# Output transposes by row halves inside the next pair's 64-row block, masked probabilities 64 bytes into their tile, new phases of batch 2

## The chip, the cores and the metric

One core of a Trainium2 chip runs the whole program. Its engines are TensorE (PE in the profile; PEld is its weight load), VectorE (DVE), ScalarE (ACT), GpSimd (POOL) and SyncE (SP, which here only starts transfers). TensorE multiplies a stationary operand (loaded as weights) with a moving one and writes to PSUM, eight banks of 2 KB per partition; DVE and ACT copy results from there to SBUF.

The metric is the device time of one execution in microseconds: the median of several runs, and beside it one profiled execution, from which all durations below come.

## The reference

Sparse attention, then a feed-forward network. There are 8 batches of 8 heads, 576 positions, 64 channels per head. Heads 0 to 3 are local: query i sees keys i-31 to i. Heads 4 to 7 are strided: query i sees keys j <= i with j = i modulo 32.

```python
scores = scale * np.matmul(q, k.transpose(0, 1, 3, 2))
mask_local = (rel >= 0) & (rel < stride)          # stride 32, rel = i - j
mask_strided = (rel >= 0) & (pos[None, :] % stride == pos[:, None] % stride)
attn = softmax(where(mask, scores, -1e9));  y = np.matmul(attn, v)
x = y.transpose(0, 2, 1, 3).reshape(B * S, H * D)  # 4608 x 512
a = x @ w1;  b = x @ w2                            # 4608 x 1024 each
out = ((a * b) @ w3) @ w_out                       # 4608 x 512
```

## The kernel before

**Network.** w3 and w_out are folded into one matrix `w34` once. The 4608 tokens go in 9 tiles of 512 (`tch`). Per tile, `ab_parts` makes for each of 8 column blocks (jc) the product aps (4 matmuls of 512 columns), which ACT copies to asb, and bps (4 more), which DVE multiplies with asb into abt (L600). `o_parts` then multiplies abt with `w34` and ACT copies the result (osb, L651) to be stored. A unit is two matmuls: 32 units of ab and 16 of o in a tile. Tile 1 has 448 new columns in its ab units, because the first 64 are done earlier.

**Attention.** Heads go in pairs (two heads fill 128 channels), four pairs to a batch: i = 0 and 1 local, 2 and 3 strided; pair p belongs to batch p // 4. For batches 2 to 7 each pair p runs these steps:

- The block (`ph_TS`, scores L334, transposes L291 and L299). All of its matmuls contract over 64 rows, alternating between the lower and the upper row half of the array. First the scores of pair p, from `qT` and `kT`; then the transposes of the next pair's q and k. In the block that precedes a batch's first pair (`rest` true) also the last 64 rows of that batch's q and k, for all heads. Scores go to the PSUM tile sps (two banks), the last chunk and the transposes to pt (two banks). A local pair has six chunks of keys with 128, 96, 96, 96, 96 and 64 queries; a strided pair has four groups of 126 and one of 72, with the positions reordered by their remainder.
- `ph_soft`: ACT takes the exp (L359) of sps, then of pt; DVE multiplies with the mask into ptm (L348), a tile that lives throughout. After it come the copies of the next pair's qT and kT.
- `ph_PV` (L368): ptm as weights against v, which has a column of ones, back into sps; `norm` on DVE divides by the sums (L525, L526) into xqs.
- `ph_T2` (L535): whole-row transposes of xqs, five or six, into psM, a pool of one bank; then copies to `xT`, the network's input. A local pair's copy is one on DVE (L540), a strided pair's one on ACT and one on DVE (L547, L548).

**Order.** TensorE's order is written out; the other engines' instructions are placed by a planner, mostly in the order of the text. A list `stream` holds the steps with gaps between them, and `host` puts one network unit of the tile into each gap (in batch 2, before its last 24 gaps, 16 units into 18). Tile `tch` hosts batch `tch + 1`. Each pair is block, 6 gaps, PV, 5 gaps, T2, 1 gap, and a batch ends with its fourth pair; the next tile's ab units start there. The first block of batch 2 and five units are placed by hand ahead of that, with seven stream entries skipped.

Batches 0 and 1 run earlier, through functions whose names begin with `ah_`, and use `ph_T2` as well. PSUM is full: psF has 3 banks for the network, psB two tiles of two banks (sps and pt), psM one bank.

Of the kernel before, what the change touches and what calls it, by code (L numbers as in the profile page):

```python
# [19 lines left out]
def kernel(  # L20
# [11 lines left out]
    nc = tc.nc  # L32
# [19 lines left out]
    NR = S - NM  # L52
    KW = 640
    NB = 512
    LC = 384
    QL = (0, 128, 224, 320, 416, 512, S)
    QX = (0, 126, 252, 378, 504, S)
    PTW = 1280
    NW, NC, NQ = 144, 4, 640
    QN = (0, 144, 288, 432, 576, NQ)  # L60

# [23 lines left out]
    def copy(eng, out, in_):  # L85
        if eng == "a":
            return nc.scalar.copy(out=out, in_=in_)  # L87
        elif eng == "v":
# [1 line left out]
        return nc.gpsimd.tensor_copy(out=out, in_=in_)  # L90


    id16 = consts.tile([P, P], FP16)
    make_identity(nc, id16)


    maskL = consts.tile([P, S], FP16)
    maskX = consts.tile([XW, S], FP16)
    biasN = consts.tile([P, NQ], FP16)
    emb = consts.tile([P, 2, 640], FP16)  # L100
# [3 lines left out]
    nc.gpsimd.memset(causal, 1.0)  # L104
    nc.gpsimd.affine_select(out=causal, in_=causal, compare_op=ALU.is_ge,
                            fill=0.0, base=0, pattern=[[1, NW]], channel_multiplier=-1)
    setup["p"] = nc.gpsimd.affine_select(out=maskL[:, 0:P], in_=causal[:, 0:P], compare_op=ALU.is_ge,
                                         fill=0.0, base=31, pattern=[[-1, P]], channel_multiplier=1)
    nptms = [ffn.tile([P, 2, 2048], FP16, tag="abt", bufs=4, name="nptm0")]
    nc.gpsimd.memset(emb, 0.0)  # L110
# [6 lines left out]
                              in_=_ap(id16, 0, [[id16.ap[0][0], m], [0, n], [1, m]]))  # L117
        pe(nc.tensor.matmul(mps[0:w, lo:lo + n * m], sel[:, 0:w], sel, start=True, stop=True))
    for i in range(1, LT):
        nc.vector.tensor_copy(out=maskL[:, QL[i]:QL[i + 1]], in_=maskL[:, 32:32 + QL[i + 1] - QL[i]])  # L120
    maskN = tmp2[:, 0:NQ]
    nc.vector.memset(maskN[:, NC * NW:NQ], 0.0)
    nc.vector.tensor_mul(maskN[:, 0:NW], mps[:, 208:208 + NW], causal)
    nc.vector.tensor_mul(maskN[0:64, NC * NW:NQ], mps[0:64, 352:416], causal[0:64, 0:64])
    nc.vector.tensor_copy(out=maskN[:, NW:NC * NW].rearrange("p (c x) -> p c x", x=NW),
                          in_=_ap(maskN, 0, [[maskN.ap[0][0], P], [0, NC - 1], [1, NW]]))
    biasL = tmp[:, S:2 * S]
    for bias, mask in ((biasL, maskL), (biasN, maskN)):
        nc.vector.tensor_scalar(out=bias, in0=mask, scalar1=1.0, scalar2=BIG, op0=ALU.subtract, op1=ALU.mult)
# [144 lines left out]
    def rest_X(eng, t, pr):  # L274
        for g in range(2):
# [3 lines left out]
        copy(eng, t[:, 2:4, XC + 64:S].rearrange("x g (s c) -> x g s c", c=4),  # L279
             pr.rearrange("x g (s a c) -> x g s a c", s=2, c=4)[:, :, :, 7])  # L280

    def ph_T(s, rest, pt):
        ps = pt.bitcast(FP16)
        h0 = 2 * (s.hp % 2)
        for i, nm in enumerate("qk"):
            src = x16[(s.b, nm, s.hp // 2)]
            for c in range(4):
                c0 = i * 256 + c * 64
                for u in range(2):
                    r = half_rows(u)  # L290
                    pe(nc.tensor.transpose(ps[:, u, c0:c0 + 64],  # L291
                                           src[r, c, h0:h0 + 2].rearrange("p h d -> p (h d)"), id16[r, r]))
        if rest:
            src = x16[(s.b, "r")]
            for g in range(4):
                c0 = 512 + g * 64
                for u in range(2):
                    r = half_rows(u)
                    pe(nc.tensor.transpose(ps[:, u, c0:c0 + 64],  # L299
                                           src[r, 2 * g:2 * g + 2].rearrange("p h d -> p (h d)"), id16[r, r]))  # L300
        engs = (("a", qT), ("v" if s.local else "a", kT))

        def out():
            for i, (eng, t) in enumerate(engs):
                pi = ps[:, :, i * 256:i * 256 + 256]
                if s.local:
                    copy(eng, t[:, s.hp, 0:NM].rearrange("x (u p c) -> x u p c", u=2, c=4),
                         pi.rearrange("x u (c p) -> x u p c", c=4))
                else:
                    to = t[:, s.hp, 0:XC].rearrange("x (c w) -> x c w", w=XW)  # L310
                    for u in range(2):
                        copy(eng, to[:, :, 56 * u:56 * u + 56].rearrange("x c (t a) -> x c t a", a=7),
                             pi[:, u].rearrange("x (c t a) -> x c t a", c=4, a=8)[:, :, :, 0:7])
                    copy("v", t[:, s.hp, XC:XC + 64].rearrange("x (u t c) -> x u t c", u=2, c=4),
                         pi.rearrange("x u (c t a) -> x u t c a", c=4, a=8)[:, :, :, :, 7])
            if rest:
                for i, (eng, t) in enumerate((("a", qT), ("v", kT))):
                    pr = ps[:, i, 512:768].rearrange("x (g r) -> x g r", g=4)
                    copy(eng, t[:, 0:2, NM:S], pr[:, 0:2])
                    rest_X(eng, t, pr[:, 2:4])  # L320

        return out

    def ph_S(s):
        w, n, q = s.w, s.n, s.q
        sps = psB.tile([P, 2, NB], FP32, tag="big", name="sps")
        pt = psB.tile([P, 2, NB], FP32, tag="big", name="pt")
        s.ps = sps

        def sc(h, c):  # L330
            r = half_rows(h)
            l = q[c + 1] - q[c]
            o = sps[:, h, q[c]:q[c + 1]] if c < n - 1 else pt[:, h, LC:LC + l]
            pe(nc.tensor.matmul(o, kT[r, s.hp, w * c:w * c + P], qT[r, s.hp, q[c]:q[c + 1]],  # L334
                                start=True, stop=True))

        for i in range(n):
            sc(0, (i - 1) % n)
            sc(1, i)

        def soft():
            ph_soft(s, pt)

        return pt, soft

    def mask_mul(s, o, i, lo, hi, m):
        x = hi - lo
# [3 lines left out]
    def ph_soft(s, pt):  # L351
        kr, q, n = s.kr, s.q, s.n
        sps = s.ps
        pte = att.tile([P, 2 * S], FP16, tag="pte", bufs=2)
        ptm = s.ptm = ptms[s.hp % 2]
        pv = pte.rearrange("p (h x) -> p h x", h=2)
        m = q[n - 1]
        for lo, hi, src in ((0, m, sps[0:kr, 0:2, 0:m]), (m, S, pt[0:kr, :, LC:LC + S - m])):
            nc.scalar.activation(out=pv[0:kr, :, lo:hi], in_=src, func=AF.Exp, bias=0.0, scale=scale)  # L359
        mask_mul(s, ptm[0:kr, 0:2 * S], pte[0:kr], 0, S, 2)  # L360

    def ph_PV(s):
        n = s.n
        s.xqs = att.tile([P, LT, 2, D], FP16, tag="xqs", bufs=2, name="xqs")
        for c in range(n):
            for h in range(2):
                c0 = h * S + s.q[c]
                pe(nc.tensor.matmul(s.ps[:, h, c * 65:c * 65 + 65], s.ptm[0:s.kr, c0:c0 + P],  # L368
                                    s.v[0:s.kr, 2 * (s.hp % 2) + h, c, :], start=True, stop=True))
        norm(s, s.ps[0:s.kr, :, 0:n * 65], 0, n)  # L370

    def ah_T1(s, i, dst=None):
        if dst is None:
# [72 lines left out]
    def ah_scores(s, g, outs, kn, first):  # L446
        w, q = s.w, s.q
        cs, lo, hi = ah_group(s, g)
        for c in cs:
            for h in range(2):  # L450
                r = half_rows(h)
                mv = qT[r, s.hp, q[c]:q[c + 1]] if q[c] < S else \
                    qT[r, s.hp].rearrange("x (c w) -> x w c", w=NW)[:, P:NW]
                pe(nc.tensor.matmul(outs[h][0:kn, q[c] - lo:q[c + 1] - lo], kT[r, s.hp, w * c:w * c + kn],  # L454
                                    mv, start=first, stop=first or c == cs[-1]))

    def ah_bias(s, g, wide=True):
        kr = s.kr
# [60 lines left out]
        norm(s, xps[0:s.kr, :, 0:len(cs) * 65], cs[0], len(cs))  # L519

    def norm(s, xv, c0, l):
        w = s.kr
        rcp = att.tile([P, 2, LT], FP32, tag="rcp")
        xv = xv.rearrange("p h (i e) -> p h i e", e=65)
        nc.vector.reciprocal(out=rcp[0:w, :, 0:l], in_=xv[:, :, :, D])  # L525
# [3 lines left out]
    def ph_T2(s):  # L529
        n = s.n  # L530
        ps = psM.tile([P, 1024], FP16, tag="m")
        for t in range(n):
            l = max(min(s.q[t + 1] - s.q[t], P), YW)
            o = t * P if s.nat else s.q[t]
            pe(nc.tensor.transpose(ps[:, o:o + l],  # L535
                                   s.xqs[0:l, t].rearrange("p h d -> p (h d)"),
                                   id16[0:l, 0:l]))
        o = xT[s.hp][:, S * s.b:S * s.b + S]
        if s.local:
            copy("a" if s.b < AHEAD else "v", o, ps[:, 0:S])  # L540
        elif s.nat:
            nc.scalar.copy(out=o[:, 0:NM].rearrange("x (p c) -> x p c", c=4),  # L542
                           in_=ps[:, 0:NM].rearrange("x (c p) -> x p c", c=4))
            nc.vector.tensor_copy(out=o[:, NM:S], in_=ps[:, NM:S])
        else:
            ov = o.rearrange("x (t a c) -> x t a c", a=8, c=4)
            nc.scalar.copy(out=ov[:, :, 0:7], in_=ps[:, 0:XC].rearrange("x (c t a) -> x t a c", c=4, a=7))  # L547
            nc.vector.tensor_copy(out=ov[:, :, 7], in_=ps[:, XC:S].rearrange("x (t c) -> x t c", c=4))  # L548


    abts = {}
    fine = []
# [154 lines left out]
    def gaps(n):  # L707
        stream.extend([GAP] * n)

    def ph_TS(s, t):  # L710
        if s is not None:
            pt, soft = ph_S(s)
            after = [soft]
        else:
            pt = psB.tile([P, 2, NB], FP32, tag="big", name="pt")
            after = []
        if t is not None:
            after.append(ph_T(t, t.hp == 0, pt))
        for f in after:
            f()  # L720

# [72 lines left out]
    add(b3, 0, 1, 2, 3)  # L794
    batch_end[0] = len(stream)

    for p, s in enumerate(pairs):
        b, i = divmod(p, 4)
        if b < AHEAD:
            continue  # L800
        t = pairs[p + 1] if p + 1 < len(pairs) else None
        add(ph_TS, s, t)
        gaps(6)
        add(ph_PV, s)
        gaps(5)
        add(ph_T2, s)
        gaps(1)
        if i == 3:
            batch_end[b] = len(stream)
    pos = [0]  # L810

    def host(units, upto):
# [146 lines left out]
```

## Time and profile before

| what | value |
|---|---|
| median of 3 runs (275.81, 274.43, 275.63) | 275.63 us |
| profiled execution, time | 273.37 us |
| profiled execution, first to last instruction | 271.5 us |
| busy: PE, DVE, ACT, POOL | 260.0, 146.7, 147.1, 99.5 us |
| mean granted TensorE clock | 0.999 |
| first block of batch 2 | at 71.54 us |
| last output transposes | at 225.9 us |

Times in the profile count from the first instruction. A busy PE is not PE at its peak, since records of successive matmuls overlap: what a step costs PE is read from the start of its first matmul to the start of the next step's. In the timeline a line is a run of like instructions: start, length, engine, line, operation, output and inputs, sizes, count, and in brackets the idle time ahead of it with what ended it.

### The profile page before, as it was taken

The numbers are of one execution on the slowest core, as the hardware profiler recorded it, in microseconds if no ns is written. First come the engines' busy times: TensorE is split into PE (matmuls) and PEld (weight loads), VectorE is DVE, ScalarE is ACT, GpSimd is POOL, SyncE is SP. The second block draws the span as 40 slices with busy tenths as digits, with TensorE's granted clock in tenths as the row PEclk, the third lists the DMA queues.
The fourth block names the chain that finished last, engine by engine and source line by source line (L and its number), as shares of the span: only waits on it lengthen the run. The fifth ranks groups of instructions, "written<-read, shape, count | busy, mean of one in ns | idle before, by whom it ended". The sixth has DMA issues, their size and how long they took to land.

```text
span 271.5 us, 6432 instructions
## 1 busy us (share of the span) xinstructions
PE 260.0 (96%) x2516; PEld 139.1 (51%) x2516; DVE 146.7 (54%) x327; ACT 147.1 (54%) x311; POOL 99.5 (37%) x119
## 2 busy tenths in 40 slices
PE   2999999999999999999999999999999999999994
PEld 1764465655645555555555555555555554444442
DVE  6472543275777557745764765477647743321320
ACT  2773334678546656566566566656675644333322
POOL 5477776678438105711750175037300000000000
PEclk9999999999999999999999999999999999999999
DMA  7999999998797249627933992399320012012003
GB/s 207 281 358 394 393 410 294 233 257 234 204 304 210 107 142 256 188 96 249 255 100 118 239 245 83 125 266 223 109 116 2 0 43 114 0 41 116 0 27 129
DMA packets 61098, 48.65 MB, mean 179 GB/s; under 512 B 31804, under 2 KB 52492, under 8 KB 61068
## 3 DMA queue, kind: packets, MB, share of 16 engines
q1 hardware_dynamic: 57036, 40.97, 54.6%
q10 hardware_dynamic: 4032, 7.28, 7.0%
q8 instruction: 19, 0.31, 0.5%
q14 instruction: 11, 0.09, 0.1%
HBM read 38.80 MB, written 9.44 MB: 178 GB/s over the span
## 4 chain that ended last, share of the span: by engine, by line
PE 90%; DVE 4%; ACT 3%; issue 1%; DVEq 0%
PE ops L640 27%; PE aps L588 22%; PE bps L597 21%; PE ps L535 3%; PE sps L368 3%; PE pt L291 2%; PE sps L334 2%; PE tps L378 2%; PE sps L466 1%; PE sps L454 1%; PE pt L334 1%; PE trp L685 1%; DVE xqs L526 1%; PE xpl L511 1%; ACT xT L542 1%
## 5 line engine op out<-in xcount | busy, mean ns | idle before, releaser
L597 PE MATMUL bps<-xT,w2h 128*128 128x512 f16 (+1 forms) x288 | 74.5, 376 | 0.0
L588 PE MATMUL aps<-xT,w1h 128*128 128x512 f16 (+1 forms) x288 | 73.9, 377 | 0.5 <-ACT xT L542 0.5
L90 POOL CAST t<-st 128x1024 f16<-128x1024 f32 (+1 forms) x46 | 46.9, 1023 | 69.6 <-DMA st<-in_q_dram 46.0
L640 PE MATMUL ops<-w,abt 128*128 128x512 f16 x280 | 67.0, 379 | 0.0
L600 DVE TENSOR_TENSOR abt<-bps,asb 128x512 f16<-128x512 f32 (+1 forms) x72 | 48.6, 678 | 32.1 <-PE bps L597 29.6
L87 ACT COPY asb<-aps 128x512 f32<-128x512 f32 (+1 forms) x71 | 42.0, 593 | 44.0 <-PE aps L588 41.1
L588 PEld LDWEIGHTS <-w1h 128*128 128x128 f16 x288 | 26.2, 98 | 29.0 <-issue 1.0
L597 PEld LDWEIGHTS <-w2h 128*128 128x128 f16 x288 | 26.3, 98 | 27.1 <-issue 0.5
L640 PEld LDWEIGHTS <-abt 128*128 128x128 f16 x280 | 25.2, 98 | 25.8
L651 ACT COPY osb<-ops 128x512 f32<-128x512 f32 x35 | 20.6, 588 | 18.5 <-PE ops L640 17.4
L359 ACT ACTIVATE pte<-sps 128x1024 f16<-128x1024 f32 (+1 forms) x24 | 24.6, 1027 | 10.6 <-PE sps L334 10.6
L526 DVE TENSOR_TENSOR xqs<-sps,rcp 128x768 f16<-128x768 f32 (+1 forms) x24 | 21.4, 890 | 0.8
L348 DVE TENSOR_TENSOR ptm<-pte,maskL 128x1152 f16<-128x1152 f16 (+2 forms) x16 | 13.0, 820 | 12.6 <-ACT pte L359 12.3
L87 ACT COPY qT<-pt 128x224 f16<-128x224 f16 (+4 forms) x60 | 18.0, 362 | 2.1 <-ACT osb L651 2.1
L348 DVE TENSOR_TENSOR ptm<-pte,maskX 126x1152 f16<-126x1152 f16 x12 | 11.7, 972 | 13.6 <-ACT pte L359 13.6
L547 ACT COPY xT<-ps 128x504 f16<-128x504 f16 x12 | 6.9, 578 | 16.5 <-PE ps L535 16.5
L89 DVE COPY kT<-pt 128x512 f16<-128x512 f16 (+4 forms) x48 | 14.1, 325 | 3.3 <-ACT kT L87 1.6
L227 POOL CAST v16L<-st 96x768 f16<-96x768 f32 x16 | 13.2, 824 | 7.0 <-DMA st<-in_v_dram 3.6
L535 PEld LDWEIGHTS <-xqs 96*128 96x128 f16 (+3 forms) x176 | 11.6, 97 | 8.2 <-DVE xqs L526 1.7
L640 PE MATMUL ops<-woh,w3T 128*128 128x512 f16 x64 | 15.6, 379 | 0.0
L535 PE MATMUL ps<-id,xqs 96*128 96x96 f16 (+3 forms) x176 | 13.6, 210 | 1.0 <-DVE xqs L526 0.9
L368 PEld LDWEIGHTS <-ptm 128*128 128x128 f16 (+1 forms) x264 | 11.0, 98 | 6.4 <-DVE ptm L348 1.9
(112 smaller groups left out, 259.0 us busy)
## 6 DMA issues: line engine op xcount, KB each, us to landing
st<-in_q_dram SPq DMA_DIRECT2D x16, 512.0 KB, 5.0
st<-in_k_dram SPq DMA_DIRECT2D x16, 512.0 KB, 6.0
st<-in_moe_w_dram SPq DMA_DIRECT2D x16, 512.0 KB, 10.4
out_dram<-osb ACTq DMA_DIRECT2D x27, 256.0 KB, 2.0
st<-in_v_dram SPq DMA_DIRECT2D x32, 144.0 KB
st<-in_v_dram SPq DMA_DIRECT2D x24, 112.0 KB, 2.4
st<-in_moe_w_out_dram SPq DMA_DIRECT2D x4, 512.0 KB, 11.8
out_dram<-osb SPq DMA_DIRECT2D x8, 256.0 KB, 4.3
```

Of the source, the lines that this page charges most:

```text
L87: return nc.scalar.copy(out=out, in_=in_)
L90: return nc.gpsimd.tensor_copy(out=out, in_=in_)
L348: nc.vector.tensor_mul(o.rearrange("p (a x) -> p a x", x=x), i.rearrange("p (a x) -> p a x", x=x), _ap(s.mask, lo, [[s.mask.ap[0][0], s.kr ...
L359: nc.scalar.activation(out=pv[0:kr, :, lo:hi], in_=src, func=AF.Exp, bias=0.0, scale=scale)
L368: pe(nc.tensor.matmul(s.ps[:, h, c * 65:c * 65 + 65], s.ptm[0:s.kr, c0:c0 + P], s.v[0:s.kr, 2 * (s.hp % 2) + h, c, :], start=True, stop=True))
L526: nc.vector.tensor_mul(s.xqs[0:w, c0:c0 + l].rearrange("p i h d -> p h i d"), xv[:, :, :, 0:D], _ap(rcp, 0, [[rcp.ap[0][0], w], [LT, 2], [ ...
L535: pe(nc.tensor.transpose(ps[:, o:o + l], s.xqs[0:l, t].rearrange("p h d -> p (h d)"), id16[0:l, 0:l]))
L588: pe(nc.tensor.matmul(st["a"][:, 0:nt], w1h[:, ci, bass.ds(jc * P, P)], xT[ci][:, tok], start=(ci == 0), stop=(ci == KM - 1)))
L597: pe(nc.tensor.matmul(st["b"][:, 0:nt], w2h[:, ci, bass.ds(jc * P, P)], xT[ci][:, tok], start=(ci == 0), stop=(ci == KM - 1)))
L600: nc.vector.tensor_mul(abts[tch][:, jc, skip:], st["b"][:, 0:nt], st["asb"][:, 0:nt])
L640: pe(nc.tensor.matmul(st["ps"], lhs(ci), rhs(ci), start=(ci == 0), stop=(ci == KF - 1)))
L651: nc.scalar.copy(out=osb, in_=ps)
```

## The change

- `ph_T2` as a step of its own goes for all pairs of batches 2 to 7 but the last. In its place `ph_T2u` transposes the 64-row halves of the previous pair's xqs at the head of the next block: the lower half into the psM bank, the upper half into a free part of pt's second bank. Twelve half transposes for a local pair, ten for a strided one. The lower half's copy to xT is issued at once, the upper half's after the block. Copies are on DVE (a strided pair has four), except for the local pairs of batch 2, on ACT.
- For 64-row halves to hold whole groups, the rows are shifted. A local pair's first chunk is rotated, queries 32 to 127 before 0 to 31, so its score matmul is split in two (`q_parts`). A strided pair's weights in PV are read from one element earlier (28 for its last group), so its rows stand at 1 to 126; `norm` then covers 128 partitions. The masked probabilities start 32 elements (64 bytes) into ptm. The mask tile and the identity are widened to give the rotated order.
- The last 64 rows of q and k of batches 3 to 7 leave the block. A new step `ph_R` does them with four whole transposes into psM, three gaps after the fourth pair's PV, with four copies on ACT and four on DVE.
- The gaps: block, 6, PV, 6 for each pair; in batch 2 (8, 7), (7, 6), (5, 4), (5, 4). In a batch's fourth pair three of the second number lie ahead of `ph_R`. A batch now ends two gaps after the next batch's first block.

```diff
-    LC = 384
+    LC = 416
+    PT0 = 32
-    PTW = 1280
+    PTW = 1248
-    id16 = consts.tile([P, P], FP16)
+    idw = consts.tile([P, 2 * P - 32], FP16)
+    id16 = idw[:, 0:P]
-    maskL = consts.tile([P, S], FP16)
+    maskE = consts.tile([P, S + 32], FP16)
+    maskL = maskE[:, 32:S + 32]
...
+        lo = 0 if i == 1 else 32
+        nc.vector.tensor_copy(out=maskE[:, QL[i] + lo:QL[i + 1] + 32], in_=maskE[:, lo:32 + QL[i + 1] - QL[i]])
...
+    nc.vector.tensor_copy(out=idw[:, P:2 * P - 32], in_=id16[:, 0:P - 32])
...
+    def q_parts(s, c):
+        if s.local and c == 0:
+            return (32, P, 0), (0, 32, P - 32)
+        return (0, s.q[c + 1] - s.q[c], 0),
+
-    def ph_S(s):
+    def ph_S(s, r):
...
+        after = [ph_T2u(r, pt)] if r is not None else []
...
-            pe(nc.tensor.matmul(o, kT[r, s.hp, w * c:w * c + P], qT[r, s.hp, q[c]:q[c + 1]],
-                                start=True, stop=True))
+            for lo, hi, at in q_parts(s, c):
+                pe(nc.tensor.matmul(o[:, at:at + hi - lo], kT[r, s.hp, w * c:w * c + P],
+                                    qT[r, s.hp, q[c] + lo:q[c] + hi], start=True, stop=True))
...
-        mask_mul(s, ptm[0:kr, 0:2 * S], pte[0:kr], 0, S, 2)
+        mask_mul(s, ptm[0:kr, PT0:PT0 + 2 * S], pte[0:kr], 0, S, 2)
+
+    def row0(s, c):
+        return 0 if s.local else 1 if c < XN else 28
...
-                c0 = h * S + s.q[c]
+                c0 = PT0 + h * S + s.q[c] - row0(s, c)
...
+    def ph_T2u(s, pt):
+        o = xT[s.hp][:, S * s.b:S * s.b + S]
+        dst = [psM.tile([P, 1024], FP16, tag="m", name="t2a"), pt.bitcast(FP16)[:, 1, 512:1024]]
+
+        def tr(u, c, o):
+            r = half_rows(u)
+            pe(nc.tensor.transpose(dst[u][:, o:o + 64], s.xqs[r, c].rearrange("p h d -> p (h d)"), id16[r, r]))
+
+        if s.local:
+            tr(0, 0, 0)
+            tr(1, 0, 0)
+            for c in range(LT):
+                if c:
+                    tr(0, c, 64 * c)
+                if c + 1 < LT:
+                    tr(1, c, 32 * c + 64)
...
+        else:
+            for c in range(XN + 1):
+                for u in range(2):
+                    tr(u, c, 64 * c)
...
+        def out(u):
+            copy("a" if s.b == AHEAD and s.local else "v", outs[u], ins[u])
+            if tails:
+                nc.vector.tensor_copy(out=tails[u][0], in_=tails[u][1])
+
+        out(0)
+        return lambda: out(1)
+
+    def ph_R(b):
+        ps = psM.tile([P, 1024], FP16, tag="m", name="rps")
+        src = x16[(b, "r")]
+        for g in range(4):
+            pe(nc.tensor.transpose(ps[:, g * P:g * P + P], src[:, 2 * g:2 * g + 2].rearrange("p h d -> p (h d)"), id16))
+        pv = ps[:, 0:NM].rearrange("x (g i r) -> x i g r", g=4, i=2)
+        rest_copies([pv[:, 0], pv[:, 1]])
...
-            after.append(ph_T(t, t.hp == 0, pt))
+            after.append(ph_T(t, t.hp == 0 and t.b == AHEAD, pt))
...
+    GAPS = ((8, 7), (7, 6), (5, 4), (5, 4))
...
-        add(ph_TS, s, t)
-        gaps(6)
+        more = p + 1 < len(pairs)
+        g = GAPS[i] if b == AHEAD else (6, 6)
+        add(ph_TS, s, pairs[p + 1] if more else None, pairs[p - 1] if p > 4 * AHEAD else None)
+        gaps(2)
+        if i == 0:
+            batch_end[b - 1] = len(stream)
+        gaps(g[0] - 2)
         add(ph_PV, s)
-        gaps(5)
-        add(ph_T2, s)
-        gaps(1)
-        if i == 3:
-            batch_end[b] = len(stream)
+        gaps(3)
+        if i == 3 and more:
+            add(ph_R, b + 1)
+        gaps(g[1] - 3 if more else 2)
+    add(ph_T2, pairs[-1])
+    gaps(1)
+    batch_end[B - 1] = len(stream)
```

## The prediction

> **What bounds the kernel now.** I read the page's busy shares first, then the chain that ended last, then TensorE's timeline over single pairs, then the waits and the DVE and ACT timelines around the steps that move.
>
> ```profile
> PE 260.0 (96%) x2516; PEld 139.1 (51%) x2516; DVE 146.7 (54%) x327; ACT 147.1 (54%) x311; POOL 99.5 (37%) x119
> ...
> PE 90%; DVE 4%; ACT 3%; issue 1%; DVEq 0%
> ```
>
> TensorE (PE) is the bound: 90% of the chain. A cut counts only where PE issues less or waits less. The timeline of one local and one strided pair of batch 5, start and length in us:
>
> ```profile
> 154.37 0.43 PE L535 MATMUL ps<-id,xqs 128*128 128x128 f16 x6
> 154.63 0.60 PE L597 MATMUL bps<-xT,w2h 128*128 128x512 f16 x2
> 155.16 0.20 PE L334 MATMUL pt<-qT,kT 64*128 64x64 f16 x1
> ...
> 155.43 0.40 PE L291 MATMUL pt<-id,t 64*128 64x64 f16 x16
> 155.75 1.04 PE L588 MATMUL aps<-xT,w1h 128*128 128x512 f16 x4
> ...
> 168.39 0.39 PE L291 MATMUL pt<-id,t 64*128 64x64 f16 x16
> 168.62 0.28 PE L299 MATMUL pt<-id,t 64*128 64x64 f16 x8
> 168.84 2.76 PE L640 MATMUL ops<-w,abt 128*128 128x512 f16 x12
> 171.44 0.47 PE L368 MATMUL sps<-v16X,ptm 126*128 126x65 f16 x10
> 171.74 2.32 PE L640 MATMUL ops<-w,abt 128*128 128x512 f16 x10
> 173.90 0.42 PE L535 MATMUL ps<-id,xqs 126*128 126x126 f16 x5
> 174.16 0.60 PE L640 MATMUL ops<-w,abt 128*128 128x512 f16 x2
> ```
>
> Starts are what to compare, since records overlap. The output transposes (L535) cost 154.63-154.37 = 0.26 us, a strided pair's five also 0.26. Sixteen half-row transposes cost 168.62-168.39 = 0.23, or 14.4 ns each, because the two row halves run side by side. A 512-column product takes (173.90-171.74)/10 = 0.216, so a unit of two takes 0.43. Two of them after 154.63 end at 155.06 and the block starts at 155.16: entering the 64-row block costs 0.10. After it, eight halves (0.115) and the exit fill 168.62 to 168.84: another 0.10. The change leaves the number of blocks at 24.
>
> From batch 3 on PE never loses 0.12 us between two starts. Batch 2 is where it does:
>
> ```profile
> 76.06 0.54 PE L588 MATMUL aps<-xT,w1h 128*128 128x448 f16 x2
> 76.97 0.44 PE L535 MATMUL ps<-id,xqs 128*128 128x128 f16 x6 [0.36 <-DVE xqs L526]
> ...
> 79.84 0.54 PE L597 MATMUL bps<-xT,w2h 128*128 128x448 f16 x2
> 80.64 0.54 PE L368 MATMUL sps<-v16L,ptm 128*128 128x65 f16 x12 [0.26 <-DVE ptm L348]
> ...
> 82.15 0.92 PE L597 MATMUL bps<-xT,w2h 128*128 128x448 f16 x4
> 83.58 0.43 PE L535 MATMUL ps<-id,xqs 128*128 128x128 f16 x6 [0.51 <-DVE xqs L526]
> ```
>
> Here a 448-column product takes 0.188. Start to start the three lose 0.53, 0.42 and 0.68: 1.63 us together.
>
> **The change, part by part.** All sums are against the profiled execution, 273.37 us (span 271.5); it lies 2.26 below the median of the three runs, 275.63, and I carry the difference over to that median. About 0.5% (1.4 us) is what a measurement of this kernel can tell from no change.
>
> Output transposes. Twenty-three pairs (8 to 30: 12 local, 11 strided) lose a step of 0.26 and gain halves in the next block: 12 for a local pair (0.173, and 0.015 because the order begins with one half twice), 10 for a strided one (0.144). That is 12 x 0.072 + 11 x 0.116 = 2.14 us less. The last pair keeps its whole-row step. Bounds: -2.3 if every half pairs, -1.3 if a half costs as much as a score matmul (12 in 155.16 to 155.43, 22 ns), which also go in both row halves. I take the 64-column transposes, being the same operation.
>
> Remaining rows. For batches 3 to 7 eight halves leave the block (0.115) and four whole transposes of 128 columns come back in their own step: 512 columns at 0.26/584 us each (the local step's columns) = 0.23. Five times +0.113 is +0.56. It is PE work with no cover.
>
> Split score matmul. Each local pair's first chunk becomes 96 and 32 columns for two heads: two more loads and matmuls in 12 blocks and 4 earlier pairs. The columns stay the same, so at least 0; at most 2 x 22 ns. I take 15 ns, near the two 14.4 ns halves less the columns moved: +0.24 (0 to 0.7).
>
> Setup. One DVE copy of 96 columns and 32 wider mask columns, ahead of the bias that PE waits for (L466 on L129, 0.2 us). The mask copies L120 are 0.1 apart: +0.1 (0 to 0.3, as k's data comes late anyway).
>
> So PE's own work: -2.14 + 0.56 + 0.24 + 0.10 = -1.24.
>
> Waits. Every block now begins with halves (0.15 to 0.19), so scores, exp and mask come that much later, and so does PV, whose distance in units is the same from batch 3 on. I call the pairs of a batch i = 0 to 3. Before, mask results were ready 0.57 to 0.75 ahead of PV in nearly all local pairs and in the second strided one, which covers this. The first strided pair (i=2) is tight: where POOL works beside it, the mask product takes 1.17 to 1.47 in place of 0.76 and ends 0.06 to 0.34 ahead of PV. Also i=1 and i=2 now start in the middle of a hidden column block (10 and 22 units in, not 12 and 24), so ACT has an asb copy (0.58) ahead of the exp. Queued behind the late exp on ACT are the qT copies and the next asb; PE waits for PV first. Bounds: 0 to 0.5 a batch; I take 0.06, since the exp itself starts only some 0.05 later than its scores allow: +0.3.
>
> xT. The strided pair's copies go from ACT (0.58) plus DVE (0.20) to four on DVE, some 1.0 us by the 0.68 of the 512-element kT copy. They end about 1.45 after the block starts; PE reads that xT 0.74 + 0.86 + 0.65 = 2.25 after (rest of the block, two units, three products). Covered; if DVE is 0.8 late, it costs the excess once a batch. On DVE's queue the mask product stands behind them, but its exp ends only at 1.9.
>
> The single psM bank. The block's first halves need the bank that the remaining rows' step filled, so PE waits for that step's eight copies.
>
> ```profile
> 167.79 0.58 ACT L547 COPY xT<-ps 128x504 f16<-128x504 f16 x1 [1.88 <-PE ps L535]
> ...
> 171.77 0.56 ACT L87 COPY qT<-pt 128x128 f16<-128x128 f16 x4 [0.41 <-ACT osb L651]
> ```
>
> ```profile
> 168.40 0.20 DVE L548 COPY xT<-ps 128x72 f16<-128x72 f16 x1 [1.14 <-ACT xT L547]
> ...
> 172.94 0.53 DVE L89 COPY kT<-pt 128x128 f16<-128x128 f16 x4
> ```
>
> L548 starts 0.03 after ACT's copy from the same bank ends, though its transposes were long done: two engines take turns. So from the step's start: 0.23, 0.20 until ACT starts (from the end of such transposes, 167.59, to 167.79), 0.56, 0.03, 0.53 = 1.55. With three units after it the block's halves come at 0.23 + 1.30 + 0.10 = 1.63: no wait (bounds 0 to 0.55 if ACT first does an osb copy). In batch 2 only one unit lies between: 0.76, so PE waits 0.8.
>
> The Trainium skill, PSUM, section on bank collisions, says that two engines may not be in one bank at the same time; the trace agrees by L548's 0.03 us. Without that rule the copies would run side by side, end at 1.0, and the wait in batch 2 would be 0.25, the sum 0.55 lower.
>
> Batch 2's phases. The 1.63 go as such: both xqs waits since those transposes move seven and six units on, the PV wait since it gets seven. What is late next: pair 9's mask ended 2.87 after its block; xT's two copies now stand on ACT ahead of its exp (0.3 to 0.6), PV comes at 3.1: wait 0.25. Pair 10 had its mask at 2.65 and PV at 2.88; PV now comes at about 2.7 (five gaps), the mask at about 3.0: 0.35. Pair 9's xqs came 2.88 after its PV; the block now takes it at 2.64 or later: 0.1. With the 0.8: 1.5 (bounds 0 to 2.5). Net -0.13.
>
> Sum: -1.24 - 0.13 + 0.3 = -1.1. Profiled 272.3; on the median 274.5 us.
>
> **The rivals.**
> (a) No new waits: the phases of batch 2 cost nothing and every mask is in time. For it: before, PE had no wait from batch 3 on. Against it: the 0.76 against 1.55 in batch 2. Time: -1.24 - 1.63 = -2.9, 272.7.
> (b) Slower: the mask products lose their place. In i=1 and i=2 the product abt (L600, 0.69) is now ready about 1.8 after the block, the mask product at 2.05; if DVE takes abt first, the mask ends 0.47 later: at 3.7 against PV at 3.4 in i=2, and just late in i=1 with POOL beside it. Some 0.45 a batch, five batches: +2.25 in place of 0.3, so +0.9 in all: 276.5. It decides from 0.27 a batch. Against: at 73.36 DVE took the mask product ahead of an abt that was as ready.
> (c) The psM wait at each boundary: ACT does an osb copy (0.59) first, so four more waits of 0.55 and 0.55 more in batch 2: +2.75 - 1.1, 277.3.
> (d) The strided pairs' probabilities are now loaded as weights from an odd element: 8 of 10 loads, 12 pairs, 96 loads. No row shows an odd start; ten PV products take 0.30, so the loads (98 ns each) are hidden. The slowest load, of 126, 64 or 72 columns at the setup (L118), took 179: +81 x 96 = 7.8, 282.3; half hidden 278.4. Below, 0.
>
> ```profile
> L118 PEld LDWEIGHTS <-tmp x4: 101/148/179, 3.9 to 4.4; 8*128 8x128 f16 x1, 32*64 32x64 f16 x1, 7*126 7x126 f16 x1, 4*72 4x72 f16 x1
> ```
>
> The Trainium skill, TensorE: Matmul & The Clock Gate, on weight-path modes, gives the fast load to 128 columns and has it read 32 bits at a time; L118's times agree on the columns, and on an odd start it names no price.
>
> **How the numbers follow.** Forecast 0.47, with its own range 273.3 to 275.4 (0.17 of it faster by over 0.5%, 0.30 within); (a) 0.25, faster; (b) 0.13, (c) 0.08, (d) 0.07, all slower. Faster 0.42, same 0.30, slower 0.28. The range holds the forecast, (a), (b) and (c): 272.0 to 277.4.
>
> **What would show it.** Right: block starts to scores 0.15 to 0.19 later; L535 only up to batch 1 and in the last pair; PE stalls in batch 2 before the block of pair 12. Wrong: PV waiting on the mask in i=2, blocks waiting on rps at each boundary, strided PV over 0.31 per ten. The prediction falls if half transposes in the block cost over 22 ns each, or if batch 2 loses over 2.5 us.

## The result and the profile after

| | before | changed |
|---|---|---|
| median of 17 runs each | 274.48 us | 273.30 us |
| profiled execution | 273.37 us | 272.68 us |
| first to last instruction | 271.5 us | 271.0 us |

The ratio is 0.9955, with a 95% interval of 0.9938 to 0.9973: 1.24 us faster (0.0045 x 274.48; the two medians differ by 1.18), more than chance, less than 0.5%. The forecast stood on the first three runs of before, whose median of 275.63 lies 1.15 above that of all 17; what can be compared is the gain, 1.1 forecast against 1.24.

The changed kernel's page, busy shares and chain:

```profile
PE 259.7 (96%) x2655; PEld 138.1 (51%) x2655; DVE 153.9 (57%) x369; ACT 142.2 (52%) x304; POOL 98.2 (36%) x119
...
PE 91%; ACT 3%; DMA 2%; DVE 1%; issue 1%; SPq 0%; ACTq 0%
```

TensorE is the bound as before, with 139 more matmuls and 0.3 us less busy time; DVE has taken on 7 us. The starts of the tiles' first aps products in PE's timeline cut the two profiles into stretches (us; "again" is a second profile of each kernel, from the experiments):

| stretch | before | before again | changed | changed again |
|---|---|---|---|---|
| start to tile 1's first product | 69.05 | 69.17 | 70.27 | 70.84 |
| tile 1 (hosts batch 2) | 28.08 | 29.28 | 27.90 | 28.03 |
| tiles 2 to 5 | 104.22 | 104.28 | 103.15 | 103.36 |
| tile 6 | 25.00 | 25.00 | 24.78 | 24.78 |
| tiles 7 and 8, to the last matmul | 41.62 | 41.62 | 41.62 | 41.62 |
| last stores | 3.56 | 3.56 | 3.24 | 3.26 |

The steady tiles gain, 25.77 in place of 26.05. Tile 1, for which the new gaps were made, gives 0.18 between the first profiles and 1.25 between the second ones, where it was the kernel before that lost more. The start has lost more than a microsecond that nobody forecast. The last stores end 0.3 earlier: their instructions are the same, and why they land sooner stays open.

The steady tiles in PE's timeline of the changed kernel (start, length in us):

```profile
101.99 1.03 PE L656 MATMUL aps<-xT,w1h 128*128 128x512 f16 x4
102.95 0.20 PE L577 MATMUL t2a<-idw,xqs 64*128 64x64 f16 x1
102.95 0.20 PE L577 MATMUL pt<-idw,xqs 64*128 64x64 f16 x1
...
103.14 0.19 PE L348 MATMUL pt<-qT,kT 64*128 64x64 f16 x1
103.14 0.42 PE L348 MATMUL sps<-qT,kT 64*128 64x96 f16 x12
...
103.40 0.40 PE L301 MATMUL pt<-idw,t 64*128 64x64 f16 x16
103.73 1.04 PE L665 MATMUL bps<-xT,w2h 128*128 128x512 f16 x4
...
115.75 0.20 PE L577 MATMUL t2a<-idw,xqs 64*128 64x64 f16 x1
...
115.91 0.19 PE L348 MATMUL pt<-qT,kT 64*128 64x72 f16 x1
...
119.10 0.47 PE L383 MATMUL sps<-v16X,ptm 126*128 126x65 f16 x10
119.41 1.46 PE L708 MATMUL ops<-w,abt 128*128 128x512 f16 x6
120.70 0.39 PE L615 MATMUL rps<-idw,t 128*128 128x128 f16 x4
120.93 1.46 PE L708 MATMUL ops<-w,abt 128*128 128x512 f16 x6
122.32 0.20 PE L577 MATMUL t2a<-idw,xqs 64*128 64x64 f16 x1
```

A local pair's twelve halves take 103.14 - 102.95 = 0.19, a strided pair's ten 0.16, in place of 0.26 each. Lower and upper half start together (both at 102.95). The scores, now 14 matmuls, take 103.14 to 103.40 = 0.26; before, twelve took 0.27. The remaining rows take 0.23. Six products from 120.93 end at 122.22 and the block follows 0.10 later: no wait on psM.

Batch 2, the same view:

```profile
87.19 0.59 PE L708 MATMUL ops<-w,abt 128*128 128x512 f16 x2
87.93 0.48 PE L383 MATMUL sps<-v16X,ptm 126*128 126x65 f16 x10
...
94.59 0.39 PE L615 MATMUL rps<-idw,t 128*128 128x128 f16 x4
94.82 0.59 PE L708 MATMUL ops<-w,abt 128*128 128x512 f16 x2
96.55 0.20 PE L577 MATMUL t2a<-idw,xqs 64*128 64x64 f16 x1 [1.14 <-DVE kT L90]
```

The old waits are gone, but pair 10's PV starts 0.31 late (two products from 87.19 end at 87.62), and pair 12's block starts 1.30 after the last product ends at 95.25, 0.10 of it the entry. ACT's timeline there, and DVE's:

```profile
94.36 0.58 ACT L719 COPY osb<-ops 128x512 f32<-128x512 f32 x1 [1.42 <-PE ops L708]
94.98 0.34 ACTq L723 DMA_DIRECT2D out_dram<-osb  x1
95.36 0.56 ACT L88 COPY qT<-rps 128x128 f16<-128x128 f16 x4 [0.41 <-PE rps L615]
```

```profile
95.95 0.54 DVE L90 COPY kT<-rps 128x128 f16<-128x128 f16 x4 [1.37 <-ACT qT L88]
```

ACT copies osb and issues its store until 95.32 before it turns to the bank whose transposes ended at about 94.82; DVE waits for ACT, PE for DVE, whose copies end at 96.49.

### The profile page after: what moved, and what is told of

Same layout as the page of the kernel before. It is cut to its first block, busy times and chain, and to the rows that moved or that the text cites. A ratio compares the mean times of both kernels' runs of the same rounds, so it can differ in the third digit from the quotient of the medians.

```text
span 271.0 us, 6732 instructions
## 1 busy us (share of the span) xinstructions
PE 259.7 (96%) x2655; PEld 138.1 (51%) x2655; DVE 153.9 (57%) x369; ACT 142.2 (52%) x304; POOL 98.2 (36%) x119
## 4 chain that ended last, share of the span: by engine, by line
PE 91%; ACT 3%; DMA 2%; DVE 1%; issue 1%; SPq 0%; ACTq 0%
PE ops L708 27%; PE bps L665 23%; PE aps L656 22%; PE sps L383 3%; PE t2a L577 2%; PE pt L301 2%; PE sps L348 2%; DMA st<-in_k_dram 2%; PE tps L393 2%; PE sps L471 1%; PE sps L483 1%; PE ps L551 1%; PE trp L753 1%; PE xpl L528 1%; ACT xT L562 1%
## 5 line engine op out<-in xcount | busy, mean ns | idle before, releaser
L665 PE MATMUL bps<-xT,w2h 128*128 128x512 f16 (+1 forms) x288 | 73.1, 376 | 0.0
L91 POOL CAST t<-st 128x1024 f16<-128x1024 f32 (+1 forms) x46 | 45.3, 994 | 68.5 <-DMA st<-in_q_dram 43.5
L665 PEld LDWEIGHTS <-w2h 128*128 128x128 f16 x288 | 27.1, 98 | 31.0 <-issue 0.7
L656 PEld LDWEIGHTS <-w1h 128*128 128x128 f16 x288 | 26.5, 98 | 28.9 <-issue 1.3
L360 DVE TENSOR_TENSOR ptm<-pte,maskE 128x1152 f16<-128x1152 f16 (+2 forms) x16 | 12.1, 765 | 7.5 <-ACT pte L371 6.7
L88 ACT COPY qT<-pt 128x224 f16<-128x224 f16 (+4 forms) x40 | 15.0, 425 | 0.2 <-PE pt L309 0.2
L90 DVE COPY kT<-pt 128x512 f16<-128x512 f16 (+4 forms) x28 | 11.4, 417 | 6.5 <-ACT kT L88 4.7
L360 DVE TENSOR_TENSOR ptm<-pte,maskX 126x1152 f16<-126x1152 f16 x12 | 10.2, 852 | 8.4 <-ACT pte L371 8.4
L260 POOL CAST v16X<-st 126x1024 f16<-126x1024 f32 x6 | 6.8, 1133 | 17.5 <-DMA st<-in_v_dram 17.5
L91 POOL COPY v16L<-v16L 32x640 f16<-32x640 f16 x16 | 12.4, 779 | 1.0
L90 DVE COPY xT<-t2a 128x252 f16<-128x252 f16 (+1 forms) x21 | 8.2, 390 | 8.0 <-PE t2a L577 7.8
```

Source lines behind the costliest of these rows:

```text
L90: return nc.vector.tensor_copy(out=out, in_=in_)
L360: nc.vector.tensor_mul(o.rearrange("p (a x) -> p a x", x=x), i.rearrange("p (a x) -> p a x", x=x), _ap(s.mask, lo, [[s.mask.ap[0][0], s.kr ...
L656: pe(nc.tensor.matmul(st["a"][:, 0:nt], w1h[:, ci, bass.ds(jc * P, P)], xT[ci][:, tok], start=(ci == 0), stop=(ci == KM - 1)))
L665: pe(nc.tensor.matmul(st["b"][:, 0:nt], w2h[:, ci, bass.ds(jc * P, P)], xT[ci][:, tok], start=(ci == 0), stop=(ci == KM - 1)))
```

## The experiments

All edits are to the changed kernel. "Lost" is the time from one matmul's start to the next less the first one's own columns.

### The start: 72 rows again

```diff
-                tr(t, s.q[t + 1] - s.q[t], s.q[t], 0 if t else P - 32)
+                tr(t, max(s.q[t + 1] - s.q[t], YW), s.q[t], 0 if t else P - 32)
```

> The changed kernel with one edit: in the whole-row output transposes of batches 0 and 1 a local pair's last chunk goes with 72 rows, as before the change, in place of 64. Theory (64 rows put this one transpose into the 64-row mode, and TensorE pays an entry and an exit of 0.10 us each, four times): in the changed kernel's trace the four steps run 0.38 to 0.46 us from start to start against 0.21 to 0.34 before; with 72 rows they fall back, the first product of tile 1 comes 0.4 to 0.8 us earlier than the changed kernel's 70.27 us, and the tiles after it are unchanged (25.8 us). Rival (the later start of tile 1, 70.27 against 69.05 us, is all set-up work and the granted clock of that run): the first product of tile 1 stays within 0.15 us of 70.27 once the clock's start is allowed for.

The step of pair 4 in PE's timeline, in the changed kernel and in this one:

```profile
64.59 0.52 PE L551 MATMUL ps<-idw,xqs 128*128 128x128 f16 x6
65.05 1.04 PE L708 MATMUL ops<-w,abt 128*128 128x512 f16 x4
```

```profile
64.96 0.42 PE L551 MATMUL ps<-idw,xqs 128*128 128x128 f16 x6
65.22 1.03 PE L708 MATMUL ops<-w,abt 128*128 128x512 f16 x4
```

0.46 becomes 0.26. All four steps fall back, from 0.45, 0.53, 0.45 and 0.46 to 0.26, 0.34, 0.26 and 0.26. From tile 0's first product to tile 1's it is 50.23 us in place of 50.65 (before: 50.24), and from the first such step to tile 0's first product 1.72 in place of 1.91 (before: 1.72). So 0.6 us of the start is this one transpose of 64 rows, four times. Tile 1's first product nevertheless came at 70.23, not 0.4 to 0.8 earlier as expected: in this execution the first PV started 0.57 later than in the changed kernel's (15.82 against 15.25), which the section on the kernel before takes up. The ratio to the kernel before was 0.9945 (0.9922 to 0.9969), no different from the changed kernel's; an edit of 0.6 us is read from the trace here, not from the times of the runs. And tiles 3 and 4 took 26.05 and 26.48, though nothing in them was edited; that is taken up under POOL's casts.

### The psM wait: remaining rows earlier in batch 2

```diff
-        gaps(3)
+        lead = 1 if b == AHEAD and i == 3 else 3
+        gaps(lead)
         if i == 3 and more:
             add(ph_R, b + 1)
-        gaps(g[1] - 3 if more else 2)
+        gaps(g[1] - lead if more else 2)
```

> The changed kernel with one edit: in batch 2 the remaining rows' step stands one gap after the fourth pair's PV in place of three, so three units lie between it and the next block in place of one. Theory (the block waits for the one psM bank until ACT's four and then DVE's four copies are done, 1.55 us after the step starts and 0.4 more where ACT first copies osb and issues its store): the block of pair 12 starts without the 1.2 us wait, and tile 1's first product to tile 2's first product takes 26.7 to 26.9 us in place of 27.90; overall 1.0 to 1.2 us faster than the changed kernel. Rival (the wait is for DVE's backlog of that pair, its normalisation above all, and not for the distance): 0.5 us or more of the wait stays.

PE's timeline of this kernel:

```profile
93.44 0.39 PE L615 MATMUL rps<-idw,t 128*128 128x128 f16 x4
93.66 1.46 PE L708 MATMUL ops<-w,abt 128*128 128x512 f16 x6
95.06 0.20 PE L577 MATMUL t2a<-idw,xqs 64*128 64x64 f16 x1
```

Six products end at 94.96, and the block starts 0.10 later: no wait is left. The stretch took 26.69 in place of 27.90, 1.21 less, as the distance theory has it. 271.76 us (4 runs), a ratio of 0.9895 (0.9853 to 0.9937).

### Are the new gaps worth anything? Batch 2 with the others' gaps

```diff
-    GAPS = ((8, 7), (7, 6), (5, 4), (5, 4))
+    GAPS = ((6, 6), (6, 6), (6, 6), (6, 6))
```

> The changed kernel with one edit: batch 2 has the gaps of all other batches, (6, 6) for each pair, in place of (8, 7), (7, 6), (5, 4), (5, 4). Theory (with the output transposes moved into the next block the xqs waits of batch 2 are gone whatever the gaps, and the new gaps only add the wait on psM and on pair 10's mask): the 1.3 and 0.31 us lost before pair 12's block and pair 10's PV vanish, pair 9's PV waits about 0.2 and its block up to 0.45 for xqs, and tile 1's first product to tile 2's first takes 26.6 to 27.3 us in place of 27.90. Rival (the new gaps are what removed batch 2's waits): the waits before pair 9's block and PV come back with 0.5 us each or more, and the stretch takes 27.9 us or longer.

PE's timeline of this kernel, the three places with idle time in batch 2:

```profile
78.07 0.20 PE L577 MATMUL t2a<-idw,xqs 64*128 64x64 f16 x1 [0.37 <-DVE xqs L543]
...
81.11 0.54 PE L383 MATMUL sps<-v16L,ptm 128*128 128x65 f16 x12 [0.19 <-DVE ptm L360]
...
86.51 0.48 PE L383 MATMUL sps<-v16X,ptm 126*128 126x65 f16 x10 [0.20 <-DVE ptm L360]
```

Start to start they lose 0.53 (entry included), 0.36 and 0.36. The psM wait is gone, and the stretch took 27.34: less than 27.90, but above the 27.3 that my theory allowed. Neither side had it whole. The new gaps do remove 0.43 on pair 9's xqs (0.53 less the entry) and 0.36 on its mask, about 0.8 us. Pair 10's wait is there with both (0.36 here, 0.31 with the new gaps), though my theory had it vanish. And the new gaps cost 1.2 on psM, so on balance they lose. In time (273.41 us, 10 runs, ratio 0.9957, 0.9926 to 0.9988) this kernel and the changed one can't be told apart; in its profile tiles 2 to 5, which the edit does not touch, took 26.14, 25.81, 26.52 and 26.42, 1.8 us more than four times 25.77 (see under POOL's casts).

### The halves undone

```diff
-        add(ph_TS, s, pairs[p + 1] if more else None, pairs[p - 1] if p > 4 * AHEAD else None)
+        add(ph_TS, s, pairs[p + 1] if more else None, None)
...
         gaps(g[1] - 3 if more else 2)
+        if more:
+            add(ph_T2, s)
```

together with the 72 rows of the first experiment.

> The changed kernel with the row halves undone and all else kept: each pair's output transposes go by whole rows in a step of their own, right ahead of the next block (72 rows for a local pair's last chunk, so no change of mode). Shifted rows, split scores, the remaining rows' step and the gaps stay. Theory (the halves are the gain: a local pair's step 0.26 against 0.18 in the block, a strided pair's 0.26 against 0.15): each tile from 2 on takes 0.36 to 0.40 us more than the changed kernel's 25.77, that is 26.15, and 2.1 us more in all, less the 0.6 that the 72 rows give back before tile 1. Rival (the halves cost the block as much as the step did, and the gain comes from the rest of the change): the tiles stay within 0.1 us of 25.77.

Slower than forecast: 277.55 us (4 runs), a ratio of 1.0101 (1.0065 to 1.0138) to the kernel before, and tiles 3 to 5 took 26.56 each, 0.79 more than 25.77 and twice the 0.38 expected (tile 2, where a POOL cast also drew out a mask product to 1.54, took 27.34). PE's and ACT's timelines of this kernel around pairs 17 and 18:

```profile
136.34 1.03 PE L656 MATMUL aps<-xT,w1h 128*128 128x512 f16 x4
137.20 0.43 PE L551 MATMUL ps<-idw,xqs 128*128 128x128 f16 x6
137.56 0.20 PE L348 MATMUL pt<-qT,kT 64*128 64x72 f16 x1
...
138.16 1.04 PE L665 MATMUL bps<-xT,w2h 128*128 128x512 f16 x4
...
140.76 0.47 PE L383 MATMUL sps<-v16X,ptm 126*128 126x65 f16 x10
141.25 1.02 PE L656 MATMUL aps<-xT,w1h 128*128 128x512 f16 x4
```

```profile
137.93 0.65 ACT L88 COPY xT<-ps 128x576 f16<-128x576 f16 x1
138.46 1.03 ACT L371 ACTIVATE pte<-sps 126x1008 f16<-126x1008 f32 x1
```

Step and block of a local pair's transposes take 0.96 (137.20 to 138.16) against 0.87 to 0.88 with the halves (102.85, where the four products from 101.99 end, to 103.73); a strided pair's 0.98 against 0.85. That is 2 x 0.09 + 2 x 0.13 = 0.44 a batch, the forecast's terms. The rest is waiting: after PV the aps product starts 0.18 late in pair 18 (140.76 + 0.31 = 141.07) and 0.06 late in pair 17, and the fourth pair's step starts 0.10 late (150.63), just after DVE's last copy out of the psM bank that it needs (150.57). The whole-row copy of a local pair stands on ACT here, ahead of the exp, which starts 0.90 after its scores in place of 0.46; that this is what delays abt is argued from these rows, not tried by itself. So the halves' direct worth is as forecast, and a whole-row step right ahead of the block is a worse place than the one the kernel had before.

### The changed kernel once more, and without POOL's casts

The first run is the changed kernel, not edited:

> The changed kernel, not edited, once more. Theory (where a POOL cast starts just ahead of a mask product, DVE waits for it, the mask product takes 1.2 to 1.6 us in place of 0.76, and PV or a product that needs abt's bank waits; which mask is hit changes from execution to execution): tiles 2 to 5, 25.77, 25.77, 25.83 and 25.77 us in its first profile, differ by 0.2 us or more in at least one of them, up to 26.5, while tiles 1, 6 and 7 repeat within 0.05. Rival (the longer tiles in the profiles of the edited kernels come from the edits): all tiles repeat within 0.05 us.

The other leaves out POOL's casts, and its copies within v, of later batches, and gives x16 and v16 of two batches earlier:

```diff
+            if b >= 4:
+                x16[(b, nm, grp)] = x16[(b - 2, nm, grp)]
+                continue
...
-        nc.gpsimd.tensor_copy(out=vt[0:YW, :, XN, 0:D], in_=sy)
+        if b < 4:
+            nc.gpsimd.tensor_copy(out=vt[0:YW, :, XN, 0:D], in_=sy)
```

(and likewise for the remaining rows and the other parts of v).

> The changed kernel with POOL's casts of q, k and v left out from batch 4 on, so batches 4 to 7 work on the data of two batches earlier; their transfers stay. POOL is idle from then on. Theory (POOL's casts are what lengthens the mask products): every mask product from tile 3 on takes 0.75 to 0.78 us, PE loses less than 0.12 us between any two starts there, and tiles 3 to 5 take 25.77 us each within 0.03. Rival (the longer ones come from DVE's order of work, which has more copies than before, or from the transfers): mask products over 0.9 us or waits on abt or ptm over 0.12 us remain in tiles 3 to 5.

Not edited, the kernel's tiles 2 to 5 took 25.77, 25.77, 25.92 and 25.90: they move, by 0.09 and 0.13, less than the 0.2 expected and more than the rival's 0.05, and tile 1 moved too (28.03). Without the casts all four took 25.77, and no two starts from tile 3 on were more than 0.10 too far apart (an entry). The group of mask products of that kernel, min/median/max in ns:

```profile
L370 DVE TENSOR_TENSOR ptm<-pte,maskX x12: 757/759/759, 88.0 to 222.9; 126x1152 f16<-126x1152 f16 x12
```

In the changed kernel's profile the mask products reached 1407 ns, in the 72-row one 1639. How one comes to cost PE time, in the 72-row kernel's DVE, POOL and PE timelines:

```profile
156.60 1.60 DVE L360 TENSOR_TENSOR ptm<-pte,maskE 128x1152 f16<-128x1152 f16 x1 [0.72 <-ACT pte L371]
...
158.27 0.68 DVE L668 TENSOR_TENSOR abt<-bps,asb 128x512 f16<-128x512 f32 x1
```

```profile
156.56 1.04 POOL L91 CAST t<-st 128x1024 f16<-128x1024 f32 x1 [11.23 <-PE bps L665]
```

```profile
158.26 0.54 PE L383 MATMUL sps<-v16L,ptm 128*128 128x65 f16 x12
159.00 1.02 PE L656 MATMUL aps<-xT,w1h 128*128 128x512 f16 x4 [0.19 <-DVE abt L668]
```

The cast starts 0.04 before the mask product, which then takes 1.60 in place of 0.76; abt, which is behind it, is late, and PE's next aps product, which needs a bank that abt still reads, starts 0.36 late. Over the profiles of this family of kernels, the one with whole rows aside, tile 4 took from 25.77 to 26.52 in this way. It also matters which of the two starts first: in the same kernel a mask product that started at 111.21, 0.07 before a cast, took 0.76, and the cast 1.59 in place of 1.04. The Trainium skill, SBUF, "Who interferes with whom", says that a DVE instruction with two SBUF inputs and a POOL instruction that reads SBUF exclude each other, and that the one issued first holds the port; the trace agrees, with the 0.04 us between the two starts and the 757 to 759 ns of every strided mask where POOL had nothing to do.

The kernel before meets the same casts and hardly pays for them. In its two profiles mask products of tiles 2 to 5 took up to 1.56 us, and those tiles still took 26.04 to 26.16, so each lost 0.12 us at most; in the six profiles of the changed family that keep the casts and the halves, tiles 2 to 5 together lose between 0.06 and 1.8. So the change has also taken slack from the steady tiles. Whether it is the halves at the head of the block or the blocks' new places within a column block was not tried.

### The start: before once more

> The kernel before, not edited, once more, to see how much of the 1.2 us by which tile 1 starts later in the changed kernel's profile (70.27 against 69.05 us) repeats. Theory: 0.6 us of it is the 64-row transposes of batches 0 and 1 (two steps ahead of tile 0's first product cost 0.19 us there, two ahead of tile 1's 0.41), and the other 0.6 us is the moment at which TensorE's full clock is granted, which changes from execution to execution (11.6 us in that profile, 12.3 to 14.6 in those of the changed kernels): the time from tile 0's first product to tile 1's repeats at 50.24 within 0.03, while tile 0's first product moves from 18.81 by up to 1 us with the clock. Rival (set-up work of the change costs those 0.6 us): tile 0's first product is again at 18.8 within 0.15.

Tile 0's first product came at 18.93 (18.81 in the first profile), against 19.62 and 20.20 in the changed kernel's two; from there to tile 1's it is 50.24 again. That it came within 0.15 of 18.81 is the sign that was named for the rival, and the 1 us of movement that my theory allowed did not show. So the two kernels do differ by more than the 0.2 of the 72 rows in the first 20 us, or happened to. But the rival's set-up work is not the reason: the first score matmul starts at 8.98 and 9.04 before, at 9.20 and 8.93 in the changed kernel. What differs comes after it: 128-column transposes run 0.107 us apart at first and 0.056 later, and the trace records the full clock at 11.6 and 11.9 in the kernel before, and at 12.3 to 14.6 in the seven profiles of the changed family that record it. The first PV goes with it: 14.63 where the clock came at 11.6, 14.75 at 11.9, 14.91 at 12.3, 15.12 at 13.1 and 15.8 at 14.6. Only the changed kernel's first profile is 0.2 off this order (15.25 at 12.7), and there the first score matmul was already 0.3 later than in its second. With the 0.6 of the 72 rows this accounts for the start: 15.25 - 14.63 + 0.61 = 1.23, of 1.22 measured. The Trainium skill, TensorE: Matmul & The Clock Gate, Part 1, has the gate judge the load in windows that run freely, so that the moment varies from execution to execution, by 500 ns either way; the trace agrees that it varies, but by more, 2.3 us among like kernels. Both profiles of before have it earlier than all seven of the changed family, but whether the change itself makes it later is not settled with two.

This second profile of before also lost more in batch 2. Two of its four waits in PE's timeline:

```profile
74.95 0.54 PE L368 MATMUL sps<-v16L,ptm 128*128 128x65 f16 x12 [0.47 <-DVE ptm L348]
...
81.95 0.54 PE L368 MATMUL sps<-v16L,ptm 128*128 128x65 f16 x12 [0.80 <-DVE ptm L348]
```

2.8 us in all where the first profile had 1.63. Here too POOL casts started 0.28 and 0.01 us ahead of the two pairs' mask products, which took 1.37 and 1.64. So the wait that the change takes away there is itself 1.6 to 2.8.

### The repairs joined

72 rows, the remaining rows early, and batch 2's gaps:

```diff
-    GAPS = ((8, 7), (7, 6), (5, 4), (5, 4))
+    GAPS = ((7, 7), (7, 6), (6, 4), (5, 4))
```

> Three edits to the changed kernel together: 72 rows in the whole-row transposes of batches 0 and 1, the remaining rows' step of batch 2 one gap after PV in place of three, and batch 2's gaps (7, 7), (7, 6), (6, 4), (5, 4), which give pair 10's PV one gap more and take it from pair 8. Theory: the terms add, 0.6 us ahead of tile 1, 1.2 on psM and 0.31 on pair 10's mask; tile 1's first product to tile 2's first takes 26.3 to 26.5 us against the changed kernel's 27.90, no wait over 0.2 us is left in batch 2, and the whole is 2.0 us faster than the changed kernel, a ratio of 0.986 to 0.990 against the kernel before. Rival (the gaps of batch 2 balance one wait against another): with the psM wait gone pair 8's or pair 9's mask or xqs comes late, and the stretch stays above 26.7 us.

271.12 us (6 runs), a ratio of 0.9886 (0.9852 to 0.992) to the kernel before, so about 2 us faster than the changed kernel. It has the lowest ratio of all, but its interval overlaps that of the kernel with the remaining rows early alone (0.9895), so that the two can't be told apart. Tile 1 took 26.93, not 26.3 to 26.5. One wait of 0.65 is left, on pair 10's PV; DVE's and POOL's timelines:

```profile
85.68 1.48 DVE L360 TENSOR_TENSOR ptm<-pte,maskX 126x1152 f16<-126x1152 f16 x1 [0.17 <-ACT pte L371]
```

```profile
84.52 2.02 POOL L91 CAST t<-st 128x1024 f16<-128x1024 f32 x2
```

By these rows it is not the gaps: the mask product started 0.17 after the second of POOL's casts (85.51) and took 1.48 in place of 0.76. Without the wait the tile would have taken 26.28, as expected. That gap more for pair 10 was therefore not shown to be of use.

## Why the prediction was right, point by point

- **Output transposes** (-2.14): 0.19 and 0.16 measured in the block, 0.188 and 0.144 forecast, 0.26 gone. The halves undone cost 0.44 a batch directly, and 0.35 more in waits, which that experiment's expectation did not have.
- **Remaining rows** (+0.56): 0.23 for a step, as forecast.
- **Split score matmul** (+0.24): nothing; 14 matmuls take 0.26 where twelve took 0.27. This term was mis-sized: I charged an extra load and matmul, and side by side in the two row halves they took no time that can be seen. A steady tile should gain 2 x 0.072 + 2 x 0.116 - 0.113 = 0.26 without it; tiles 2, 3 and 5 gained 0.27 to 0.30, and tile 4, which lost 0.06 in a wait, 0.21.
- **Setup** (+0.1): not seen; the first score matmul starts within 0.2 us either way.
- **What the sum left out** (+0.60): I read the change to the whole-row step as a matter of the last pair, though batches 0 and 1 use it too. There the last chunk went from 72 to 64 rows, which puts one transpose into the 64-row mode; entry and exit, 0.10 each, were in my own first view.
- **Steady waits** (+0.3): 0.06 in the first profile, 0.28 in the second (0.15 + 0.13), 1.0 in the 72-row kernel's and 1.8 in the one with uniform gaps, always with POOL's casts, or its copies within v, under a mask product. The 0.3 was right for the changed kernel's own two profiles and too small for those, whose steady tiles are the same. I had put them on the strided pairs and on DVE's order; any mask can be hit. Rival (b)'s price came near in one execution (1.8 against its 2.25), and its mechanism was wrong: DVE never took abt first in these rows, the mask product was just long.
- **xT by DVE**: four copies end 1.4 us after the block's first half (122.32 to 123.69), 1.45 forecast; PE never waited for it in the steady tiles.
- **psM at the other boundaries**: 1.62 us from the step to the block (120.70 to 122.32), 1.63 forecast, and no wait. **In batch 2**: 1.2 in place of 0.8. The sum's term was too small by ACT's osb copy and store. Rival (c) had that delay, as 0.55 at each boundary and here; it came here alone, as 0.4.
- **Batch 2's phases** (-1.63 + 1.5): 0 on pair 9's mask (0.25 forecast), 0.31 on pair 10's (0.35), 0 on xqs (0.1), 1.2 on psM (0.8). New waits 1.5, as in the sum, by errors that cancel. The waits taken away were 1.63 in the first profile of before and 2.8 in the second, so tile 1 gave 0.18 and 1.25.
- **Rival (a)**, no new waits, failed on psM as its own line said. **Rival (d)**: strided PV takes 0.31 for ten with odd starts, 0.30 to 0.31 before; their weight loads average 98.2 ns against 97.7. An odd start has no price here.

So the gain was right by a steady part that held and two errors that partly cancel: 0.34 too much for split and setup, 0.60 left out at the start. That 1.1 comes so near 1.24 is also luck. Batch 2 gave between 0.2 and 1.25, the casts took between 0.06 and 1.8 over like kernels, the last stores gave 0.3 that nothing explains, and the moment of the clock moves the start by about a microsecond.

## What to carry to other kernels

Short matmuls of one row mode belong together: moved into a block that pays its entry already, half-row transposes cost two thirds of the whole-row ones and no switch. Look for the reverse too: one operand shrunk from 72 rows to 64 costs 0.2 us each time, with nothing in the text to show it. When a step is moved away from a wait, measure which single buffer it now meets: here a distance of two gaps was worth as much as the whole change.

## What the runs showed of the hardware that I had not expected

- A lone 64-row transpose between 128-row work loses 0.10 us before it and 0.10 after (0.46 against 0.26 for the step). The Trainium skill, TensorEngine Tiling (Array Packing), Key Properties, says that a change of tiling mode drains the engine; the trace agrees that the change costs time, and here the price is these 0.20 us.
- A mask product that starts 0.04 us after a POOL cast takes 1.60 us in place of 0.76; one that starts 0.07 before a cast keeps its 0.76.
- Splitting a 128-column score matmul into 96 and 32 columns, side by side in the two row halves, took no time that can be seen (0.26 against 0.27 us for the twelve).
- The full TensorE clock was recorded between 11.6 and 14.6 us after the first instruction, and the first PV moves with it, from 14.6 to 15.8 us.
